# Spreading pooled k over two columns by ScalarE instead of GpSimd in a fused attention and expert kernel

## The chip, the cores and the metric

The kernel runs on one core of a Trainium2 chip. The metric is device time in microseconds (us) of one execution; runs of one kernel are told by their median. A core has five engines that work side by side, each through its own list of instructions in program order: TensorE (PE in the profile; PEld is its weight load), VectorE (DVE), ScalarE (ACT), GpSimd (POOL) and SyncE (SP), which issues the DMAs. An instruction waits on semaphores until what it needs is done, and all that stands behind it on the same engine waits too.

## The reference

Three stages stand behind each other. Attention with k and v averaged over groups of 8 positions, on 4 batches, 8 heads, 576 positions and 64 columns a head:

```python
Sp = S // pool                                   # 576 // 8 = 72 pooled positions
k_p = k.reshape(B, H, Sp, pool, D).mean(axis=3)
v_p = v.reshape(B, H, Sp, pool, D).mean(axis=3)
scores = scale * np.matmul(q, k_p.transpose(0, 1, 3, 2))
attn = softmax(scores)                           # the maximum subtracted, 1e-09 added to the sum
attn_out = np.matmul(attn, v_p)
```

Its result, as 2304 rows of 512, goes through four experts whose outputs are summed with weights: `out += p[:, e:e+1] * (np.maximum(x @ w1[e], 0) @ w2[e])`, and that through `((x @ g_w1) * (x @ g_w2)) @ g_w3 @ g_wout`. All is fp32.

## The kernel before, in words

Only the first stage and the first expert, which overlap in the first 200 us, matter here. Matrix products are done in three passes of a rounded format: a matrix is split into a high and a low half (`hi_lo`, lines 174 to 176: ScalarE copies the high half, VectorE or GpSimd subtracts it from the source for the low half), and `mm3` (lines 169 to 172) multiplies low by high, high by low and high by high.

The order of all work is written out by hand; the engines' lists follow the order in which the code records instructions. Attention is done in 18 tiles of 128 positions. A **lead** comes first: a list of pieces (lines 644 to 647) that pools k and v of batch 0, forms scores, exponents and normalised weights of tiles 0 to 2, and ends with the pooling of three chunks of k of batch 1 and with `attend(0)`, which makes the first 384 rows of x. After it the units of the first expert run: for 6 blocks of 384 rows and 8 column groups of 128, `expert_h` makes hidden values (12 matmuls, `g<-xl` and `g<-xh`; the result is copied by ScalarE, line 695, and VectorE, line 696), and two units later they are multiplied by w2 (9 matmuls, `g<-w2`). Between the units, `hooks` (lines 649 to 677) place the pieces of attention for the remaining tiles.

Pooled k of one batch is 8 heads x 72 positions = 576 rows, taken as five **chunks** (`NCH`), four of 128 rows and one of 64. `pool_k` sums a chunk's groups of eight: by one VectorE reduction (line 415), or, for chunks 0 to 2 of batch 1, by three GpSimd additions (lines 417 to 419). The sum `kp` (128x64, two buffers) is then spread to `kb` (128 x 2 x 64): each row appears in the half that belongs to its head's place in a pair of heads and is zero in the other, because the row is multiplied by the two columns of the mask `mk` (lines 349 to 356). The rows that the last chunk lacks are set to zero by GpSimd (line 413). TensorE transposes `kb` chunk by chunk (`make_kT`, line 429; in batch 0 with idle transposes between, line 432), and ScalarE copies the result from PSUM to kT (line 433). `scores` multiplies by it (line 503); VectorE takes the maximum (515) and subtracts it (520), ScalarE takes the exponent (518 in tiles 0 to 2, 521 later), VectorE sums and inverts (527 to 529), GpSimd or VectorE multiplies (532), TensorE transposes (541) and ScalarE copies (547). `attend` multiplies by pooled v (556) and splits the result into x (175, 176). After the lead all scores, transposed weights and transposes of k share two PSUM banks.

The five spreads of batch 0 stand in the lead, of batch 1 at the lead's end (chunks 0 to 2) and in hook 1 (chunks 3 and 4), of batches 2 and 3 in hooks 15 to 17 and 25 to 27, two chunks a hook.

Of the kernel before, what the change touches and what calls it, by code (L numbers as in the profile page):

```python
# [11 lines left out]
AF = mybir.ActivationFunctionType  # L12
ALU = mybir.AluOpType
# [4 lines left out]
def fused_kernel(  # L18
# [16 lines left out]
    nc = tc.nc  # L35
    PSUM = bass.MemoryType.PSUM

    B, H, S, D = q.shape
# [288 lines left out]
    with tc.manual_schedule():  # L327
# [27 lines left out]
        mk = ap.tile([P, NCH, 2], F32, tag="mk", name="mk", bufs=1)  # L355
# [37 lines left out]
        in_t, kb_t, kT_t, vp_t, qT_t, sc_t, e_t, sm_t, at_t = {}, {}, {}, {}, {}, {}, {}, {}, {}  # L393
# [13 lines left out]
        def pool_k(b, c, eng=nc.vector):  # L407
            if c == 0:
                kb_t[b] = ap.tile([P, NCH, 2, D], F32, tag="kb", name="kb", bufs=1)
            r, n = in_t.pop(("k", b, c))  # L410
            kp = ap.tile([P, D], F32, tag="kp", name="kp")
            if n < P:
                nc.gpsimd.memset(kb_t[b][n:, c], 0.0)
            if eng is nc.vector:
                eng.tensor_reduce(kp[:n], r[:n, :].rearrange("p (r d) -> p d r", d=D), axis=AX.X, op=ALU.add)  # L415
            else:
                eng.tensor_tensor(r[:n, :256], r[:n, :256], r[:n, 256:], op=ALU.add)
                eng.tensor_tensor(r[:n, :128], r[:n, :128], r[:n, 128:256], op=ALU.add)
                eng.tensor_tensor(kp[:n], r[:n, :64], r[:n, 64:128], op=ALU.add)
            nc.gpsimd.tensor_tensor(kb_t[b][:n, c], kp[:n].unsqueeze(1).broadcast_to([n, 2, D]),  # L420
                                    mk[:n, c].unsqueeze(2).broadcast_to([n, 2, D]), op=ALU.mult)

        def make_kT(b, g0, g1, warms=()):
            if g0 == 0:
# [167 lines left out]
        def do_k(b, on_pool=0):  # L592
            return [(("k", b, c), lambda c=c: pool_k(b, c, nc.gpsimd if c < on_pool else nc.vector)) for c in range(NCH)]
# [872 lines left out]
```

## Time and profile before

| | before |
|---|---|
| median of 3 runs | 1164.84 us (1162.38 to 1165.03) |
| the profiled execution | 1163.69 us |
| its span, first to last instruction | 1162.0 us |
| TensorE busy | 1152.0 us (99%) |
| VectorE busy | 795.9 us (68%) |
| GpSimd busy | 483.8 us (42%) |
| ScalarE busy | 381.4 us (33%) |

Busy time is from one execution taken by the hardware profiler. TensorE's busy time counts a matmul from its start to its end, and matmuls overlap, so a busy TensorE need not be at its peak. Idle time of an engine is put down to what released it. The shares of the whole span are means over stages that differ: the attention's pieces lie in the first 200 us.

### The profile page before, as it was taken

The page shows a single profiled execution, that of the slowest core. Times are in us where ns is not written, and L with a number is a line of the kernel's source. Part 1 is how long each engine was busy: PE and PEld are TensorE (multiplying, and loading weights), DVE is VectorE, ACT ScalarE, POOL GpSimd, SP SyncE. Part 2 cuts the span into 40 slices and gives each one's busy share as a digit, 9 for nine tenths or more (in the row PEclk, how much of TensorE's full clock was granted, in tenths as well). Part 3 has the DMA queues.
Part 4 walks back from the last instruction along what each step waited for, and adds up shares of the span by engine and source line. Part 5 has one row for each costly group of instructions (what it writes and reads, how often), then busy time and mean ns, then how long its engine had stood idle before and what let it go on. Part 6 is the DMA issues. An engine that isn't in the chain of part 4 may idle for free.

```text
span 1162.0 us, 19466 instructions
## 1 busy us (share of the span) xinstructions
PE 1152.0 (99%) x6834; PEld 1042.7 (90%) x6834; DVE 795.9 (68%) x1619; ACT 381.4 (33%) x704; POOL 483.8 (42%) x563
## 2 busy tenths in 40 slices
PE   8999999999999999999999999999999999999998
PEld 7888898999898998998989989889888999999998
DVE  6866553476586778667778577877677777775454
ACT  5543433245141234421315414124352333231110
POOL 6965222166452547634436745255001222342111
PEclk9999999999999999999999999999999999999999
DMA  8966434555877645768583488686475542945651
GB/s 212 214 151 142 143 103 143 186 194 179 284 242 219 217 135 155 225 185 253 182 251 103 154 241 246 153 269 145 138 184 210 204 165 113 329 164 187 233 190 46
DMA packets 233218, 217.54 MB, mean 187 GB/s; under 512 B 92960, under 2 KB 185376, under 8 KB 233120
## 3 DMA queue, kind: packets, MB, share of 16 engines
q1 hardware_dynamic: 233120, 216.30, 60.5%
q8 instruction: 54, 0.88, 0.3%
q14 instruction: 44, 0.36, 0.1%
HBM read 144.41 MB, written 71.83 MB: 186 GB/s over the span
## 4 chain that ended last, share of the span: by engine, by line
PE 93%; DVE 2%; DMA 2%; issue 1%; POOL 1%; ACT 1%; SPq 0%; POOLq 0%; DVEq 0%; ACTq 0%
PE g L171 17%; PE g L172 17%; PE g L170 17%; PE s L170 13%; PE s L171 13%; PE s L172 13%; PE x_ps L556 1%; PE sc L503 1%; DMA raw<-in_moe_w_dram 1%; PE at_ps L541 1%; DMA plain<-in_k_dram 0%; POOL w2l L176 0%; DVE ap L415 0%; POOL plain L841 0%; DMA stxl<-in_k_dram 0%
## 5 line engine op out<-in xcount | busy, mean ns | idle before, releaser
L176 POOL TENSOR_TENSOR round<-plain,round 128x576 fp32r<-128x576 f32 (+1 forms) x131 | 189.7, 1448 | 397.1 <-ACT round L175 269.0
L172 PE MATMUL s<-xo,wh 128*128 128x288 f32 x840 | 248.3, 296 | 0.0
L170 PE MATMUL s<-xo,wh 128*128 128x288 f32 x840 | 248.3, 296 | 0.0
L171 PE MATMUL s<-xo,wl 128*128 128x288 f32 x840 | 247.8, 295 | 0.0
L170 PE MATMUL g<-w2l,round 128*128 128x512 f32 x540 | 211.5, 392 | 0.0
L172 PE MATMUL g<-w2h,round 128*128 128x512 f32 x540 | 210.9, 391 | 0.0
L171 PE MATMUL g<-w2h,round 128*128 128x512 f32 x540 | 210.8, 390 | 0.1
L957 DVE TENSOR_TENSOR plain<-s,plain 128x288 f32<-128x288 f32 x320 | 137.9, 452 | 89.5 <-PE s L172 63.7
L170 PEld LDWEIGHTS s<-xo,wh 128*128 128x128 f32 x840 | 158.1, 188 | 0.7
L171 PEld LDWEIGHTS s<-xo,wl 128*128 128x128 f32 x840 | 157.7, 188 | 0.7
L172 PEld LDWEIGHTS s<-xo,wh 128*128 128x128 f32 x840 | 158.0, 188 | 0.0
L175 ACT ACTIVATE round<-plain 128x576 fp32r<-128x576 f32 (+1 forms) x135 | 90.9, 676 | 161.8 <-DVE plain L1315 158.7
L172 PEld LDWEIGHTS g<-w2h,round 128*128 128x128 f32 x540 | 101.3, 188 | 21.3
L170 PEld LDWEIGHTS g<-w2l,round 128*128 128x128 f32 x540 | 101.5, 188 | 20.4 <-issue 0.8
L171 PEld LDWEIGHTS g<-w2h,round 128*128 128x128 f32 x540 | 101.4, 188 | 20.1 <-DVE round L696 0.4
L959 ACT ACTIVATE plain<-s 128x288 f32<-128x288 f32 x80 | 32.2, 402 | 235.6 <-PE s L172 235.5
L1168 ACT ACTIVATE plain<-plain 128x576 f32<-128x576 f32 x96 | 65.4, 682 | 129.6 <-DVE plain L957 124.3
L288 POOL TENSOR_TENSOR x5l<-x5l 128x256 uint32<-128x256 uint32 x80 | 59.5, 744 | 101.1 <-DVE x5l L287 99.1
L957 DVE TENSOR_TENSOR plain<-s,pb 128x288 f32<-128x288 f32 x160 | 69.7, 455 | 26.0 <-PE s L172 14.5
L696 DVE SCALAR_TENSOR_TENSOR round<-g,round 128x384 fp32r<-128x384 f32 x48 | 26.6, 554 | 68.8 <-ACT round L695 68.5
L170 PE MATMUL g<-xl,round 128*128 128x384 f32 x192 | 66.6, 347 | 0.0
L172 PE MATMUL g<-xh,round 128*128 128x384 f32 x192 | 64.6, 336 | 0.0
(253 smaller groups left out, 2203.9 us busy)
## 6 DMA issues: line engine op xcount, KB each, us to landing
xo<-keptx SPq DMA_DIRECT2D x63, 576.0 KB
raw<-in_moe_w_dram SPq DMA_DIRECT2D x64, 256.0 KB
plain<-acc SPq DMA_DIRECT2D x40, 256.0 KB
keptx<-xo SPq DMA_DIRECT2D x16, 576.0 KB
x5h<-in_moe_w_dram SPq DMA_DIRECT2D x128, 64.0 KB
x5h<-in_moe_w_dram SPq DMA_DIRECT2D x32, 256.0 KB
kept<-xo SPq DMA_DIRECT2D x12, 576.0 KB
acc<-plain SPq DMA_DIRECT2D x26, 256.0 KB
```

Source lines behind the costliest of these rows:

```text
L170: nc.tensor.matmul(ps, lh, rl, start=first, stop=False)
L171: nc.tensor.matmul(ps, ll, rh, start=False, stop=False)
L172: nc.tensor.matmul(ps, lh, rh, start=False, stop=last)
L175: nc.scalar.activation(hi, src, AF.Copy)
L176: (lo_eng or nc.vector).tensor_tensor(lo, src, hi.bitcast(F32), op=ALU.subtract)
L288: nc.gpsimd.tensor_tensor(au, au, bu, op=ALU.add)
L503: nc.tensor.matmul(sc[off:off + n, (hp % 2) * W:(hp % 2 + 1) * W], qT[:, hp, off:off + n], kT_t[b][:, hp * W:(hp + 1) * W], start=True, st ...
L541: nc.tensor.transpose(pt[:NK, g * P:(g + 1) * P], e[:, half * G + g, :], ident)
L696: nc.vector.scalar_tensor_tensor(hl, ps, 0.0, hh.bitcast(F32), op0=ALU.max, op1=ALU.subtract)
L957: nc.vector.tensor_tensor(to, one, two, op=ALU.add)
L959: nc.scalar.activation(x, product(j, A11, B11), AF.Copy)
L1168: nc.scalar.activation(r, r, AF.Relu)
```

## The change

The last instruction of `pool_k`, the product of the pooled chunk with both mask columns at once on GpSimd, is replaced by two ScalarE instructions, one for each half, that copy the chunk with one mask column as a scale by row:

```diff
@@ pool_k
-            nc.gpsimd.tensor_tensor(kb_t[b][:n, c], kp[:n].unsqueeze(1).broadcast_to([n, 2, D]),
-                                    mk[:n, c].unsqueeze(2).broadcast_to([n, 2, D]), op=ALU.mult)
+            for a in range(2):
+                nc.scalar.activation(kb_t[b][:n, c, a], kp[:n], AF.Copy, scale=mk[:n, c, a:a + 1])
```

Twenty GpSimd instructions go, forty on ScalarE come. The zeroing of line 413 and the additions of lines 417 to 419 stay on GpSimd. TensorE, VectorE and SyncE keep their instructions in the same order. The number of table loads on ScalarE stays one.

On ScalarE at the start of the program, batch 0 (`pb` is the area that holds `kb`, `ap` the area of `kp` and kT), the difference, with + for what is new:

```order
 L1461 UNCONDITIONAL_BRANCH
-L433 ACT_TABLE_LOAD
+L421 ACT_TABLE_LOAD
+L421 ACTIVATE pb<-ap_70 128x64 x8
 L433 ACTIVATE ap_70<-kT_ps 128x512
+L421 ACTIVATE pb<-ap_70 64x64 x2
 L433 ACTIVATE ap_70<-kT_ps 128x128
 L487 ACTIVATE plain<-qT_ps 128x512
```

Eight copies (chunks 0 to 3) now stand ahead of the first copy of kT, and chunk 4's two stand behind it.

On ScalarE at the end of the lead and in the first units, before (`round<-raw` and `w2h<-raw` are high halves of weights, `xh<-x_ps` the high halves of the attention result, `round<-g` hidden values):

```order
L547 ACTIVATE ap_70<-at_ps 72x4x128 x5
L175 ACTIVATE round<-raw 128x512
L175 ACTIVATE xh<-x_ps 128x384 x4
L175 ACTIVATE round<-raw 128x512
L695 ACTIVATE round<-g_423 128x384
L175 ACTIVATE round<-raw 128x512
L175 ACTIVATE w2h<-raw 128x512
L521 ACTIVATE ap_70<-ap_70 128x288 x2
L695 ACTIVATE round<-g_472 128x384
```

and now, at the same place:

```order
L547 ACTIVATE ap_70<-at_ps 72x4x128 x5
L175 ACTIVATE round<-raw 128x512
L421 ACTIVATE pb<-ap_70 128x64 x6
L175 ACTIVATE xh<-x_ps 128x384 x4
L175 ACTIVATE round<-raw 128x512
L695 ACTIVATE round<-g_431 128x384
L175 ACTIVATE round<-raw 128x512
L175 ACTIVATE w2h<-raw 128x512
L521 ACTIVATE ap_70<-ap_70 128x288 x2
L421 ACTIVATE pb<-ap_70 128x64 x2
L421 ACTIVATE pb<-ap_70 64x64 x2
L695 ACTIVATE round<-g_482 128x384
```

The six copies of batch 1's chunks 0 to 2 came in between the weights and the four copies of the attention result, and the four of chunks 3 and 4 between the exponents and the second group of hidden values.

On ScalarE around batch 2, before:

```order
L175 ACTIVATE xh<-x_ps 128x384 x4
L521 ACTIVATE ap_70<-ap_70 128x288 x2
L695 ACTIVATE round<-g_903 128x384
L547 ACTIVATE ap_70<-at_ps 72x4x128 x2
L521 ACTIVATE ap_70<-ap_70 128x288 x2
L695 ACTIVATE round<-g_967 128x384
```

and now:

```order
L175 ACTIVATE xh<-x_ps 128x384 x4
L521 ACTIVATE ap_70<-ap_70 128x288 x2
L421 ACTIVATE pb<-ap_70 128x64 x4
L695 ACTIVATE round<-g_915 128x384
L547 ACTIVATE ap_70<-at_ps 72x4x128 x2
L421 ACTIVATE pb<-ap_70 128x64 x4
L521 ACTIVATE ap_70<-ap_70 128x288 x2
L421 ACTIVATE pb<-ap_70 64x64 x2
L695 ACTIVATE round<-g_982 128x384
```

The pairs of two chunks each came in ahead of the hidden values and ahead of the exponents, and chunk 4's pair ahead of the next hidden values; batch 3 has the same three places.

## Rows read from the trace of the kernel before

**Rows 1.** The page: busy us (share of the span) and instructions of each engine.

```profile
PE 1152.0 (99%) x6834; PEld 1042.7 (90%) x6834; DVE 795.9 (68%) x1619; ACT 381.4 (33%) x704; POOL 483.8 (42%) x563
```

**Rows 2.** Stretches: begin:end and length, busy us, granted clock, DMA share, GB/s.

```profile
25.90:36.00 10.10, 8.50 (x52) 7.58 (x50) 8.86 (x15) 6.36 (x13) 9.26 (x17) 1.00 0.68 178
36.00:60.00 24.00, 23.37 (x139) 20.61 (x140) 19.59 (x36) 11.66 (x24) 22.38 (x31) 1.00 0.99 222
60.00:80.00 20.00, 20.00 (x132) 17.72 (x131) 16.56 (x30) 8.84 (x19) 11.98 (x22) 1.00 0.59 124
```

**Rows 3.** Waits of TensorE: who for whom, us in total, times, longest.

```profile
PE kT_ps L429 <- POOL pb L420: 2.8, 6, 1.0
```

**Rows 4.** One line's instructions: ns least/median/most, first to last start.

```profile
L420 POOL TENSOR_TENSOR pb<-ap x20: 392/398/1422, 4.7 to 109.4; 128x128 f32<-128x128 f32 x16, 64x128 f32<-64x128 f32 x4
...
L518 ACT ACTIVATE ap<-sc,ap x24: 308/340/428, 12.1 to 18.8; 128x72 f32<-128x72 f32 x24
```

**Rows 5.** Timeline of the lead: start, us, engine, line, what [idle before <- releaser].

```profile
1.43 3.25 PE L637 MATMUL warm<-ident 128*128 128x128 f32 x14 [1.43 <-POOL ident masks.py:199]
...
9.52 0.60 ACT L433 ACTIVATE ap<-kT_ps 128x512 f32<-128x512 f32 x1 [7.42 <-PE kT_ps L429]
9.64 0.39 POOL L420 TENSOR_TENSOR pb<-ap 64x128 f32<-64x128 f32 x1 [0.28 <-DVE ap L415]
...
10.79 1.22 PE L503 MATMUL sc<-ap,plain 128*128 128x144 f32 x8
...
12.05 3.50 ACT L518 ACTIVATE ap<-sc,ap 128x72 f32<-128x72 f32 x16 [0.53 <-DVE ap L515]
...
18.70 1.47 PE L637 MATMUL warm<-ident 128*128 128x128 f32 x12
```

**Rows 6.** Timeline of the lead's end and the first expert matmuls.

```profile
22.97 0.62 ACT L175 ACTIVATE round<-raw 128x512 fp32r<-128x512 f32 x1
...
23.12 2.80 PE L556 MATMUL x_ps<-ap 72*64 72x384 f32 x16 [0.25 <-ACT ap L547]
...
24.02 1.28 POOL L176 TENSOR_TENSOR round<-raw,round 128x512 fp32r<-128x512 f32 x1
24.04 0.49 ACT L175 ACTIVATE xh<-x_ps 128x384 fp32r<-128x384 f32 x1 [0.45 <-PE x_ps L556]
...
24.56 2.49 DVE L176 TENSOR_TENSOR xl<-x_ps,xh 128x384 fp32r<-128x384 f32 x4
...
25.26 0.73 POOL L417 TENSOR_TENSOR stxh<-stxh 128x256 f32<-128x256 f32 x1
...
25.86 0.44 PE L170 MATMUL g<-xl,round 128*128 128x384 f32 x1
...
26.62 0.33 POOL L419 TENSOR_TENSOR ap<-stxh 128x64 f32<-128x64 f32 x1
...
28.04 1.14 PE L503 MATMUL sc<-ap 128*128 128x144 f32 x8
```

**Rows 7.** Timeline of the first units, with chunks 3 and 4 of batch 1.

```profile
31.77 2.03 DVE L415 TENSOR_REDUCE ap<-stxl 128x64 f32<-128x512 f32 x2
...
33.72 0.55 DVE L696 SCALAR_TENSOR_TENSOR round<-g,round 128x384 fp32r<-128x384 f32 x1
...
35.56 1.58 DVE L528 TENSOR_SCALAR ap<-ap 128x8 f32<-128x8 f32 x1
...
38.70 1.20 PE L503 MATMUL sc<-ap 128*64 128x144 f32 x16 [0.39 <-DVE ap L490]
```

**Rows 8.** Timeline of batch 2: VectorE, ScalarE and TensorE.

```profile
72.44 1.06 DVE L415 TENSOR_REDUCE ap<-stxh 128x64 f32<-128x512 f32 x1
...
72.58 1.07 ACT L547 ACTIVATE ap<-at_ps 72x512 f32<-72x512 f32 x2
...
74.87 1.14 PE L503 MATMUL sc<-ap 128*128 128x144 f32 x8
```

**Rows 9.** Stretches, as in Rows 2: the last three microseconds.

```profile
1159.00:1162.00 3.00, 0.00 (x0) 0.00 (x0) 0.23 (x1) 0.00 (x0) 0.00 (x0) 1.00 0.15 50
```

## The prediction

> **What bounds the kernel now.** I read the engine totals first, then the table of stretches, the waits of TensorE, and the timeline at the places where the changed line runs. TensorE is busy for 1152.0 us, 99% of the span [rows 1]: any time that it loses is time lost, and what another engine gains is worth only what TensorE had waited for it. The changed line runs in the first 110 us alone [rows 4]. There the stretches [rows 2] show TensorE short by 1.6 us between 25.9 and 36 us, by 0.6 us between 36 and 60, and by nothing from 60 to 80. GpSimd is the full engine of these stretches: 9.26 of 10.10 us, then 22.38 of 24.00. ScalarE has room: 6.36 and 11.66. So the change moves work from a full engine to one with room, and the waits of TensorE on that line, 2.8 us in six waits [rows 3], are the most it can give back directly.
>
> **What goes and what comes.** Twenty GpSimd products go. One takes 0.40 us by the median and 1.42 at worst [rows 4]. Forty ScalarE instructions of 128x64 (or 64x64) come, each with the mask column as a scale that is read from memory. No such row exists; the nearest is line 518, 128x72 with a bias read from memory: 0.34 us alone [rows 4], and sixteen of them in 3.50 us, so 0.22 apart [rows 5]. A pair is then 0.22 + 0.35 = 0.57 us, 0.17 more than the GpSimd product. Bounds are 0.40 (as before) and 0.68 (two without overlap); I take 0.57 because the row differs by eight columns and the source only. This matters little. What matters is the place: ScalarE works its instructions off in program order, so a pair that waits holds up all that stands behind it.
>
> **The lead, batch 0.** The pairs of chunks 0 to 3 follow VectorE's sums as the products did, each 0.17 us later. Then line 433 (the 512-column copy), which ran from 9.52 for 0.60 us, goes from 9.7 to 10.3, and the pair of chunk 4 stands behind it: it ends at 10.8, where the product ran from 9.64 to 10.03 [rows 5]. The first scores move from 10.79 to 11.55, +0.75. ScalarE carries this to line 175 (the high half of the first weights, 22.97 in [rows 6]), now about 23.7. GpSimd does not carry it: its pooling of v filled it until 24.02, so its subtraction of line 176 starts at about 24.4, +0.4.
>
> **The step that costs.** Batch 1's chunks 0 to 2 are pooled by GpSimd itself (lines 417 to 419). Their pairs now stand on ScalarE ahead of the four copies of line 175 that read the first attention result from PSUM (24.04 in [rows 6]). Before, those copies waited for nothing but TensorE. Now they wait until GpSimd has pooled three chunks. One chunk takes 1.69 us (25.26 to 26.62 + 0.33), 1.65 from start to start without the product between. With GpSimd's subtraction ending at 24.4 + 1.28 = 25.7, the third sum is ready at 25.7 + 3 x 1.65 = 30.65. The last pair adds 0.6: the first copy starts at 31.2, not at 24.04. It takes 0.49, the first low half on VectorE a quarter of 2.49, 0.62, two handovers 0.1: the first expert matmul starts at 32.45, not at 25.86, +6.6. Queued behind the waiting pairs are the copies, the high half of the second weight tile and line 695; VectorE's low halves and TensorE's whole queue wait for them. Since the low halves come 0.62 apart and TensorE takes 0.52 for each, the group ends at 34.85 at full rate, where the scores of tile 3 followed at 28.04: **+6.8**. Removing three products from GpSimd shortens this by 2 us; it is counted already.
>
> **The clock.** TensorE's last product ahead of the gap (23.12 + 2.80, moved by 0.75) ends at 26.7; it then idles for 5.8 us. At the start of the program fourteen transposes took 3.25 us, 0.23 each, and later twelve took 1.47, 0.12 each [rows 5]: after idleness the engine ran at the lower of its two levels, 1.2 GHz, though the granted-clock column prints 1.00 there too. In the last three microseconds TensorE does nothing, and the column still prints 1.00 [rows 9]. So the rows show three microseconds of idleness without a fall and a slow start after a long idleness; 5.8 us lies between. If it falls, the twelve matmuls of the first group take 0.35 each instead of 0.17: 4.16 us from 32.45, ending at 36.6, **+8.55** instead of +6.8. Bounds for this term are 0 and 3.3 us (two slow stretches like that of the start, half of each lost); I take 1.75, one stretch: 5.8 us is almost twice the idleness that did no harm, and the one start that the rows show was slow.
>
> The Trainium skill's page "TensorE: Matmul & The Clock Gate", section "Why this matters for your kernels", warns that a long idle gap between bursts of matmuls sends the array back to half rate. No row here shows a fall. By that rule the sum is the one with the fall; by [rows 9] alone it would be 1.75 us lower.
>
> **Up to the scores of tile 4.** Before, TensorE waited here for chunks 2, 3 and 4: 1.6 us. Chunks 0 to 2 are now ready before TensorE comes to them. Chunks 3 and 4 are summed by VectorE (31.77 for 2.03 us [rows 7], now about 40.2 to 42.2), and their pairs stand on ScalarE ahead of line 695 of the second group: 42.2 + 0.6 = 42.8, then 0.49, so VectorE's line 696, which stood at 33.72, comes at 43.25, +9.5. From there to the scores of tile 4 were 4.98 us (33.72 to 38.70), of which over 1.0 was in one tiny VectorE instruction, line 528, that lasted 1.58 us [rows 7] beside a busy GpSimd. With GpSimd freer I give 1.0 back: 47.2, **+8.5**; if not, 48.2, +9.5. So the 1.6 us that TensorE gains is given back to a new wait on the scores.
>
> **Batches 2 and 3.** VectorE sums all five chunks. The pairs of chunks 0 and 1 now stand ahead of line 695, and so of line 547, which empties two PSUM banks (72.58, 1.07 us [rows 8]). The second sum ends at 73.50; pair 0.6, line 695 0.4: line 547 runs from 74.5 to 75.6. The next scores need these banks at 74.87 and, for the second half, at 75.3: 0.25 to 0.3 us of wait. In batch 2 the same happens once more ahead of the transposes of k, because three large copies stand behind chunk 4's pair: 0.3. Together **+0.8**; bounds 0 (the slack of two units holds) and 2. The 0.6 us that TensorE missed between 36 and 60 may come back in part: -0.3.
>
> **The sum.** 8.5 + 0.8 - 0.3 = +9.0 on the profiled execution's 1163.69 us (span 1162.0 and 1.7 around it), 1172.7. That execution lies 1.15 below the median of the runs shown, 1164.84, and inside their spread, so I leave it so.
>
> **Rivals.** *The clock holds*: all as above without 1.75 us: +7.25, 1170.9. For it: three idle microseconds at full clock in [rows 9]; against it: the gap is twice as long.
>
> *The gap is made up*: the head start of the weight loads during the gap and a GpSimd with 8 us less work (20 x 0.40) would let later stages catch up. TensorE's misses after 25.9 are 1.6 + 0.6 us before 60 and none up to 80, so at most 2.2 of the gap come back, if the clock holds and the new waits all vanish: 6.6 - 2.2 = +4.4, 1168.1. Against it: TensorE has no idleness to give.
>
> *The wait spreads*: each pair waits for VectorE, VectorE waits for line 695 behind it, and a loop of waits costs every unit of batches 1 to 3 a microsecond: some 6 more, +15, 1178. Against it: [rows 2] leave ScalarE half its time from 36 to 60, and two groups of matmuls lie between a result and its use.
>
> *Faster*: GpSimd's load is what decides, and the copies of the attention result do not wait. This decides if the third pooled chunk is ready when ScalarE comes to the copies, at 24.04; then TensorE's 2.8 us [rows 3] go and the pairs cost 0.75 in the lead: -2, 1161.7. GpSimd only begins the first chunk at 25.26 and needs 5 us for three, so this is out by 6.6 us.
>
> **How the numbers follow.** The forecast 0.60; the clock holds 0.20; made up 0.10; spreads 0.07; faster 0.03. The range is 1168 to 1177: at the lower end the clock holds, batches 2 and 3 cost nothing, and 2 us more come back, which takes in half of the made-up case; at the upper end 1.0 (line 528), 1.2 (batches) and 1.5 (a second slow stretch) come on top of the forecast, with 0.6 more in the lead (pairs without overlap). That leaves out less than 0.2: the other half, the spreading waits and the faster case. A measurement of this kernel tells about 0.3% (3.5 us) from no change. Faster by more than that 0.02, within it 0.07 (the rest of the faster case and half of made up), slower 0.91.
>
> **What would show it.** In the profile after: ScalarE idle from about 24.4 to 30.6, released by GpSimd's line 419 in three steps; the copies of line 175 at 31; TensorE idle for almost 6 us just before its first expert matmul, at 32 to 33; those first matmuls 0.35 apart (clock fell) or 0.17 (held); no wait of TensorE on the transposes of batch 1; a wait of 1 to 3 us on the scores of tile 4; GpSimd busy 8 us less or more. I am wrong if the copies start before 28, or if TensorE's busy time plus its gaps does not grow by about the gap.

## The result

The changed kernel took **1172.23 us** (median of 4 runs, 1171.37 to 1174.04); the kernel before took 1164.01 beside it on the same chip (4 runs, 1162.38 to 1165.03). The ratio is 1.0074, 95% interval 1.0062 to 1.0087: slower, by 8.2 us. The forecast was 1172.7, and slower by more than 0.3% with a chance of 0.91. The profiled execution took 1172.54 us, its span is 1170.5.

The page of the changed kernel, engine totals, against [rows 1]: GpSimd has 9.3 us less to do, ScalarE 9.2 more, and TensorE is as full as before.

```profile
PE 1153.6 (99%) x6834; PEld 1044.8 (89%) x6834; DVE 794.5 (68%) x1619; ACT 390.6 (33%) x744; POOL 474.5 (41%) x543
```

The new line as a group of instructions (ns least/median/most, first to last start), against [rows 4]. The price of one is 0.336 us, and nearly constant; the GpSimd product's went up to 1.42.

```profile
L421 ACT ACTIVATE pb<-ap x40: 332/336/352, 4.5 to 118.2; 128x64 f32<-128x64 f32 x32, 64x64 f32<-64x64 f32 x8
```

Waits of TensorE, then of ScalarE, in the first 125 us of the changed kernel (who for whom: us in total, times, longest), against [rows 3]:

```profile
PE g L170 <- DVE xl L176: 6.1, 1, 6.1
PE kT_ps L429 <- ACT pb L421: 2.5, 5, 0.8
PE sc L503 <- DVE ap L490: 1.9, 1, 1.9
```

```profile
ACT pb L421 <- DVE ap L415: 14.5, 16, 2.5
ACT pb L421 <- POOL ap L419: 5.7, 3, 3.4
```

TensorE's wait for the spread, which the change could have taken away, is still there (2.5 us after 2.8): of it 1.9 us lie in batch 0 and 0.6 at the last chunk of batch 1, where 1.2 and 1.6 lay before. A new wait of 6.1 us stands ahead of the first expert matmul, and ScalarE waits 5.7 us in three steps for GpSimd's last additions. The timeline of the lead's end shows how the two are one thing (start, us, engine, line, what, [idle before <- releaser]), against [rows 6]:

```profile
23.45 0.62 ACT L175 ACTIVATE round<-raw 128x512 fp32r<-128x512 f32 x1
...
23.61 2.80 PE L556 MATMUL x_ps<-ap 72*64 72x384 f32 x16 [0.24 <-ACT ap L547]
...
24.52 1.27 POOL L176 TENSOR_TENSOR round<-raw,round 128x512 fp32r<-128x512 f32 x1
...
27.44 0.59 ACT L421 ACTIVATE pb<-ap 128x64 f32<-128x64 f32 x2 [3.37 <-POOL ap L419]
27.64 0.72 POOL L417 TENSOR_TENSOR stxh<-stxh 128x256 f32<-128x256 f32 x1 [0.24 <-DMA stxh<-in_k_dram]
...
29.32 0.59 ACT L421 ACTIVATE pb<-ap 128x64 f32<-128x64 f32 x2 [1.30 <-POOL ap L419]
...
30.57 0.32 POOL L419 TENSOR_TENSOR ap<-stxh 128x64 f32<-128x64 f32 x1
30.93 0.59 ACT L421 ACTIVATE pb<-ap 128x64 f32<-128x64 f32 x2 [1.02 <-POOL ap L419]
31.42 1.61 ACT L175 ACTIVATE xh<-x_ps 128x384 fp32r<-128x384 f32 x4
31.92 1.95 DVE L176 TENSOR_TENSOR xl<-x_ps,xh 128x384 fp32r<-128x384 f32 x4 [6.79 <-ACT xh L175]
...
32.53 0.69 PE L170 MATMUL g<-xl,round 128*128 128x384 f32 x1 [6.13 <-DVE xl L176]
...
36.54 0.85 PE L503 MATMUL sc<-ap 128*128 128x144 f32 x5
```

TensorE's attention result lies ready from 26.4 us. ScalarE has nothing to do but the three pairs, and these wait for GpSimd until 30.9; the copies of the result stand behind them. TensorE does nothing from 26.4 to 32.5.

The stretches of the changed kernel (begin:end and length, busy us of PE, PEld, DVE, ACT, POOL, granted clock, DMA share, GB/s), against [rows 2]:

```profile
29.00:30.00 1.00, 0.00 (x0) 0.00 (x0) 0.00 (x0) 0.59 (x2) 0.97 (x2) 0.93 0.27 78
30.00:31.00 1.00, 0.00 (x0) 0.00 (x0) 0.00 (x0) 0.07 (x1) 0.77 (x2) 0.50 0.39 90
32.50:36.00 3.50, 3.47 (x11) 3.47 (x12) 1.97 (x4) 1.04 (x3) 0.00 (x0) 0.50 0.15 21
36.00:44.50 8.50, 7.94 (x47) 7.38 (x46) 6.11 (x11) 5.29 (x13) 1.63 (x3) 0.96 0.58 151
44.50:60.00 15.50, 13.60 (x86) 12.12 (x85) 13.88 (x26) 7.25 (x16) 14.31 (x20) 1.00 0.84 207
60.00:80.00 20.00, 20.00 (x134) 17.85 (x133) 14.79 (x30) 9.67 (x20) 14.07 (x20) 1.00 0.80 182
```

The granted clock is 1.00 up to a little before 30 us and 0.50 from there (1.2 GHz, the lower level), still in the gap; the first eleven matmuls run at 0.50, and 36.0 to 44.5 has 0.96. The Trainium skill's page "TensorE: Matmul & The Clock Gate", section "Why this matters for your kernels", warns that a long idle gap between bursts sends the array back to half rate; this trace agrees, with 6.1 idle us and a fall in them. The runs below show that the length of the gap alone does not tell it.

The timeline of the first units, against [rows 7]:

```profile
42.22 0.59 ACT L421 ACTIVATE pb<-ap 64x64 f32<-64x64 f32 x2 [0.38 <-DVE ap L415]
...
43.21 0.56 DVE L696 SCALAR_TENSOR_TENSOR round<-g,round 128x384 fp32r<-128x384 f32 x1 [1.03 <-ACT round L695]
...
44.36 1.29 POOL L176 TENSOR_TENSOR w2l<-raw,w2h 128x512 fp32r<-128x512 f32 x1 [4.42 <-issue]
...
45.12 0.55 DVE L528 TENSOR_SCALAR ap<-ap 128x8 f32<-128x8 f32 x1
...
47.23 1.04 PE L503 MATMUL sc<-ap 128*64 128x144 f32 x13 [1.90 <-DVE ap L490]
```

To see where the time comes from, take the same matmul of TensorE in both traces and subtract the starts; the difference is the shift. The scores of tile 3 come 8.5 us later (28.04 and 36.54), those of tile 4 also 8.5 (38.70 and 47.23), the scores that stood at 55.60 come 8.1 later, those at 104.79 8.4 later, and the last matmul 8.6. Between, it falls to 7.3 (32.64 and 39.93), where TensorE no longer waits for the transposes, and the wait on the scores of tile 4 puts it back. So the whole loss is made by 37 us, and little comes or goes after 48 in these two executions.

### The profile page after: what moved, and what is told of

Same layout as the page of the kernel before. It is cut to its first block, busy times and chain, and to the rows that moved or that the text cites. A ratio compares the mean times of both kernels' runs of the same rounds, so it can differ in the third digit from the quotient of the medians.

```text
span 1170.5 us, 19486 instructions
## 1 busy us (share of the span) xinstructions
PE 1153.6 (99%) x6834; PEld 1044.8 (89%) x6834; DVE 794.5 (68%) x1619; ACT 390.6 (33%) x744; POOL 474.5 (41%) x543
## 4 chain that ended last, share of the span: by engine, by line
PE 93%; DMA 2%; DVE 2%; SPq 1%; issue 1%; POOL 1%; ACT 1%; ACTq 0%; POOLq 0%; DVEq 0%
PE g L171 17%; PE g L172 17%; PE g L170 17%; PE s L170 13%; PE s L171 13%; PE s L172 13%; PE sc L503 1%; PE x_ps L556 1%; PE at_ps L541 1%; DMA stxl<-in_v_dram 0%; SPq L472 0%; DMA stxh<-in_k_dram 0%; DMA stxh<-in_v_dram 0%; SPq L460 0%; SPq L404 0%
```

## The experiments

Theory: the three pairs of batch 1 stand on ScalarE ahead of copies that have nothing to do with them, wait there for GpSimd's pooling, and that one wait, with the clock that falls in it, is the loss. Rival: the spread costs more on ScalarE wherever it stands. A further rival for the size: the gap is all, and the clock costs nothing. Each edit is shown against the changed kernel (but for the kernel with the pairs in hook 0, which starts from the kernel before); `...` stands for lines or arguments left out. Where a condition chooses which chunks ScalarE spreads, the others are spread by GpSimd's product as before. The edits move line numbers: lines 490, 503, 520 and 528 of the kernel before are 494, 507, 524 and 532 in the kernels with such a condition. "Later" is always the start of the same TensorE matmul less that in the kernel before.

### Three pairs alone

ScalarE spreads chunks 0 to 2 of batch 1; the other seventeen spreads are GpSimd's again.

```diff
+            if b == 1 and c < 3:
+                for a in range(2):
+                    nc.scalar.activation(kb_t[b][:n, c, a], ...)
+            else:
+                nc.gpsimd.tensor_tensor(kb_t[b][:n, c], ...)
```

> Only the three chunks of batch 1 that GpSimd pools itself are spread by ScalarE; the other seventeen stay on GpSimd. Theory (wait): the loss is one wait, that of the attention result's copies behind these three pairs, so nearly all of it is here: first expert matmul at about 32.0 us, low clock behind it, 1171 to 1172 us. Rival (price): each pair is dearer than the product and pays its share of 8.2 us, 0.41 a pair: three pairs, +1.2, 1165.2.

Measured 1170.79 us (the kernel before beside it: 1164.33), ratio 1.0053 [1.0038, 1.0068]: 6.5 us of the 8.2 come with three of the twenty pairs, a little less than the 1171 to 1172 expected and far above the rival's 1165.2. The wait of the changed kernel is there, and the granted clock stands at 0.50 behind it, from 32 to 36 us (waits of TensorE in this kernel, first 125 us):

```profile
PE g L170 <- DVE xl L176: 5.8, 1, 5.8
```

### All but these three

```diff
+            if not (b == 1 and c < 3):
...
```

> The opposite: seventeen chunks on ScalarE, the three of batch 1 that GpSimd pools on GpSimd. Wait theory: the lead is 0.5 us later, chunks 3 and 4 of batch 1 hold up the second hidden group, batches 2 and 3 cost 0.2 to 0.8: 1165 to 1166.3, first expert matmul at 26.4 us. Price rival: seventeen pairs at 0.41, +7, 1171.

Measured 1165.92 us, ratio 1.0013 [1.0003, 1.0022]: 1.6 us for seventeen pairs. The rival of the price (1171) falls here too. The two parts add up to 8.1 us, the whole change to 8.2.

This kernel has no gap ahead of the first expert matmul, and yet its trace shows the low clock once. The waits of TensorE, then stretches:

```profile
PE sc L507 <- DVE ap L494: 1.9, 1, 1.9
```

```profile
39.00:40.00 1.00, 0.00 (x0) 0.00 (x0) 1.00 (x2) 0.28 (x2) 0.94 (x1) 1.00 1.07 203
40.00:41.00 1.00, 0.77 (x8) 0.80 (x10) 1.00 (x3) 0.00 (x0) 0.92 (x3) 0.66 1.12 221
41.00:43.50 2.50, 2.50 (x16) 2.12 (x13) 2.27 (x5) 0.49 (x2) 2.42 (x4) 0.50 1.06 216
```

A wait of 1.9 us on the scores of tile 4 was followed by the lower level, though TensorE had already gone on. In that execution the scores of tile 4 were 1.5 us later and the next scores 3.1. It took 1167.23 us, more than the median. The record has ten executions of this kernel with their mean granted clock: the five at 1.000 took 1164.76 to 1165.93 us (median 1165.51), the five at 0.998 or 0.999 1165.92 to 1167.48 (median 1167.04). So here a lower mean clock goes with some 1.5 us to the end of the program; it is a difference between executions, not an experiment.

### Batch 0 alone, and batches 2 and 3 alone

```diff
+            if b == 0:
...
```

> ScalarE spreads the five chunks of batch 0 alone; all others on GpSimd as before. By the prediction's terms: the first scores 0.7 later, the second weight's subtraction on GpSimd 0.4 later, the three pooled chunks of batch 1 and the wait for them 0.4 later, so +0.5 on the kernel before, not to be told from no change. Rival, that the cost lies evenly over the pairs (8.2 us by 5 of 20): +2.1.

Measured 1165.38 us (12 runs; before 1164.02), ratio 1.0013 [1.0005, 1.0022]: +1.4 us. The interval, 0.6 to 2.6 us, just leaves out the theory's +0.5 and holds the rival's +2.1, so the expectation missed: a cost of batch 0 is clear of noise. That the cost lies evenly over all pairs is out by the other runs; for these five it isn't. In the profiled execution TensorE waited less for the spread and more behind it (waits of TensorE, first 125 us):

```profile
PE sc L507 <- DVE ap L494: 1.7, 1, 1.7
PE kT_ps L433 <- ACT pb L422: 1.4, 2, 0.8
...
PE kT_ps L433 <- POOL pb L424: 0.6, 1, 0.6
```

```diff
+            if b >= 2:
...
```

> Only batches 2 and 3 (ten chunks) are spread by ScalarE; batches 0 and 1 by GpSimd as before. The forecast gave these +0.8; the changed kernel's trace, read from the scores of tile 6 to those of batch 3, gives +0.3: 1164.3 + 0.3 = 1164.6. Price rival, 0.41 a pair: 1168.4.

Measured 1165.62 us (10 runs; before 1164.22), ratio 1.0008 [0.9999, 1.0018]. By the medians that is +1.4 us, by the interval -0.1 to +2.1. The trace, of an execution that took 1163.97 us, 1.7 less than the median, shows the shift of TensorE grow from 0.2 to 0.7 us over batches 2 and 3 and fall to 0.3 at the end, with two waits on line 524 (line 520 of the kernel before), 0.6 us together. Whether the time is 0.3, 0.8 or 1.4 longer, the runs don't tell; the rival's 4.1 is out.

### The pairs behind the copies, and one pair ahead of them

If the place is what costs, moving the three pooled chunks behind `attend(0)` in the lead takes the wait away while ScalarE does the same work.

```diff
-                + weight(GP) + do_qT(3) + k1[:3] + do_attend(0) + weight(VE))
+                + weight(GP) + do_qT(3) + do_attend(0) + k1[:3] + weight(VE))
```

> As the changed kernel, but the three chunks of batch 1 are recorded behind attend(0): the copies of the attention result stand ahead of the pairs again. Wait theory: the gap ahead of the first expert matmul goes (26.4 us), but the same wait now holds the second weight tile and the first hidden group's copy until about 32.0 to 32.5, and from there VectorE's chain to the scores of tile 4 is as long as in the changed kernel (9.9 us): scores at 42.7 instead of 47.2, +4.0, 1168. Rival (the gap is all): the time falls back to 1164.5.

Measured 1167.75 us, ratio 1.0029 [1.0019, 1.0039]: 4.5 us less than the changed kernel and 3.4 more than the kernel before, near the 1168 of the theory; the rival's 1164.5 is out. The first expert matmul isn't held up any more (26.82 us), but the second weight tile now stands behind the pairs, and the scores of tile 4 come at 42.39 (42.7 expected). Waits of TensorE, then two stretches:

```profile
PE g L170 <- ACT round L175: 1.8, 1, 1.8
...
PE sc L503 <- DVE ap L490: 1.2, 1, 1.2
```

```profile
33.00:34.00 1.00, 1.00 (x6) 1.00 (x5) 1.00 (x3) 0.34 (x1) 0.59 (x1) 0.67 0.86 239
34.00:36.00 2.00, 2.00 (x8) 1.91 (x7) 1.93 (x5) 0.89 (x2) 1.04 (x2) 0.50 0.65 189
```

With one pair left ahead of the copies and two behind:

```diff
+                + weight(GP) + do_qT(3) + k1[:1] + do_attend(0) + k1[1:3] + weight(VE))
```

> As the changed kernel, but only chunk 0 of batch 1 is recorded ahead of attend(0), chunks 1 and 2 behind it. Theory (what counts is when the third pair lets line 695 of the first hidden group go, not the length of the gap): the first expert matmul starts at about 29.1 us, between 26.8 (all three behind) and 32.5 (all three ahead), but line 696 of the first group is as late as with all three behind, so the time is that of that run, 1167.8, +3.4. Rival (the gap itself is the loss): a gap of 2.5 us more than with all three behind, 1170.

Measured 1168.11 us, ratio 1.0039 [1.0025, 1.0052]. Waits of TensorE, and the two stretches behind the gap:

```profile
PE g L170 <- DVE xl L176: 2.3, 1, 2.3
PE sc L503 <- DVE ap L490: 1.9, 1, 1.9
```

```profile
26.00:29.00 3.00, 0.73 (x5) 0.47 (x4) 1.08 (x3) 2.07 (x7) 2.72 (x6) 1.00 0.71 149
29.00:40.00 11.00, 10.17 (x57) 8.83 (x56) 8.43 (x15) 7.73 (x22) 3.71 (x6) 1.00 0.68 169
```

One pair costs a gap of 2.3 us where three cost 6.1, and the time is that of the kernel with all three behind the copies, as the theory has it; the rival's 1170 lies just below the interval's upper end (1170.3), so the time alone doesn't rule it out, but the last matmul comes 3.8 us late in both. The clock holds here through the gap of 2.3 us and through the wait of 1.9, while waits of 1.8 (pairs behind the copies) and 1.9 (all but three) were followed by a fall.

### Idle transposes in the gap

To keep the clock up and leave the wait as it is, 44 idle transposes (`warm`) stand behind `attend(0)`, and in a second kernel 16 more ahead of the scores of tile 4.

```diff
+                + weight(GP) + do_qT(3) + k1[:3] + do_attend(0) + warm(44) + weight(VE))
```

> The changed kernel with 44 idle transposes (4.8 us at 0.109) on TensorE in the gap ahead of the first expert matmul. Theory (the clock adds 1.75 us to the wait): granted clock 1.00 throughout, the first group's matmuls 0.17 apart, scores of tile 3 at 34.8 instead of 36.5, scores of tile 4 at 45.5 instead of 47.2, time 1170.4. Rival (VectorE and ScalarE set the pace there, the clock costs nothing): scores of tile 4 stay at 47.2, 1172.2.

Measured 1173.64 us (1171.91 to 1173.87; the profiled execution is the fastest), ratio 1.0075 [1.006, 1.009]: no gain. In the profiled execution the clock held through the gap and fell at the next wait, behind the scores of tile 4. Why the other three took 1.7 to 2.0 us longer than it, the trace can't show.

```profile
26.00:44.00 18.00, 15.54 (x104) 14.13 (x102) 10.64 (x19) 10.87 (x28) 7.04 (x12) 1.00 0.64 149
44.00:46.00 2.00, 1.39 (x14) 1.42 (x16) 2.00 (x4) 0.00 (x0) 1.92 (x3) 0.71 1.02 238
46.00:48.00 2.00, 2.00 (x10) 1.62 (x7) 1.55 (x4) 0.73 (x2) 1.92 (x4) 0.50 0.74 206
```

Then both gaps:

```diff
+        hooks[at[TPB + 1]][:0] = warm(16)
```

> The changed kernel with idle transposes on TensorE in both of its waits: 44 ahead of the first expert matmul and 16 (1.75 us) ahead of the scores of tile 4. In the run with the first 44 alone the low level only moved: it stood 3.4 us behind the scores of tile 4 instead of 4.2 us of work behind the gap. Theory (the low level is what costs): no low stretch from 20 to 60 us, scores of tile 4 at 44.6 and full rate behind them, 1170.0 to 1170.5. Rival (the time is set by VectorE's chain, the low level is only seen beside it): 1172 to 1173.6, as with the first 44.

Measured 1171.56 us, ratio 1.0063 [1.005, 1.0077], an interval that overlaps the changed kernel's. It reaches from 1170.0 to 1173.2 us, which holds both the theory's time and the lower part of the rival's, so this run decides nothing; all four of its times, 1171.09 to 1171.75, lie between the two. The same kernel and the changed one were then run side by side, five times each:

> The changed kernel once more, beside the next one on the same chip. Every theory: 1171.4 to 1174, as when it was timed first; scores of tile 4 near 47.2 us, a low level of the clock behind 29.9 us.

> The kernel with idle transposes in both gaps once more, beside the changed kernel. Theory that the low level of the clock is paid once and kept to the end: 1.8 us less than the changed kernel in the same call, both in the median and in the shift of TensorE's last matmuls. Rival, that a later wait takes it back (as the 1.2 us near 322 us did in the first execution): medians less than 1 us apart, though the shift up to 105 us is 1.8 us or more smaller. If the interval of the two overlaps and the late wait is absent, neither is shown.

Changed kernel 1171.69 us, ratio 1.0071 [1.0059, 1.0083]; both gaps warm 1171.83 us, 1.0068 [1.0056, 1.008]. Stretches of the changed kernel in this execution:

```profile
27.00:36.00 9.00, 5.03 (x18) 5.04 (x19) 2.82 (x6) 4.00 (x11) 2.09 (x5) 0.62 0.37 94
36.00:45.50 9.50, 7.54 (x43) 6.50 (x41) 8.26 (x15) 6.28 (x16) 3.81 (x4) 1.00 0.73 162
45.50:49.50 4.00, 3.84 (x22) 3.49 (x23) 3.02 (x7) 0.89 (x2) 3.84 (x6) 0.57 0.87 212
```

and of the kernel with both gaps warm:

```profile
27.00:36.00 9.00, 7.35 (x57) 7.12 (x55) 3.48 (x7) 5.25 (x14) 3.20 (x7) 1.00 0.53 135
36.00:45.50 9.50, 8.68 (x60) 7.74 (x60) 8.26 (x15) 5.61 (x15) 4.45 (x5) 1.00 0.83 187
45.50:49.50 4.00, 4.00 (x30) 3.62 (x26) 2.72 (x6) 1.76 (x4) 3.71 (x6) 1.00 0.59 179
```

From the first expert matmul to the scores of tile 4 the changed kernel takes 14.70 us in its first execution and 14.69 in its second; with the gap warm it takes 12.88, and with both 12.92 and 12.91. So the lower level costs 1.8 us there: the two executions with the fall and the three without it differ by that. It is complete at the scores of tile 3 (4.01 and 4.00 us with the fall, 2.22, 2.22 and 2.20 without). In these two runs the scores that stood at 104.79 come 8.4 us late in the changed kernel and 6.3 with both gaps warm. But then the saving shrinks: the kernel with both gaps warm, in both of its executions, meets one more wait near 329 us (waits of TensorE, 300 to 340 us):

```profile
PE s L170 <- DVE plain L1240: 0.6, 1, 0.6
```

There VectorE's chain of another stage, which works on tiles that arrive by DMA, comes last. The end is 7.7 us late against 8.6. The medians lie 0.14 us apart, as the rival has it, and the late wait is there, of 0.6 or 0.9 us; that it alone takes the saving back isn't shown, for it is smaller than 1.8. Why VectorE is late there only in this kernel, and where the rest goes between the profiled executions and the medians, stays open.

### The pairs in the first hook

This starts from the kernel before: only the three pooled chunks are spread by ScalarE, in hook 0, behind the copies and behind the second weight tile; the sums get a third buffer.

```diff
+            if b == 1 and c < 3:
+                kp_t[c] = kp
+                return
...
+        def spread_k(c):
+            for a in range(2):
+                nc.scalar.activation(kb_t[1][:, c, a], kp_t[c], AF.Copy, scale=mk[:, c, a:a + 1])
...
+        hooks[0] = [(None, lambda c=c: spread_k(c)) for c in range(3)]
```

> The kernel before, with one edit: chunks 0 to 2 of batch 1 are pooled by GpSimd in the lead, but spread by ScalarE only in hook 0, behind the first hidden group's copy and the first w2 weights, with a third buffer for the sums. No copy waits for GpSimd, and GpSimd has three products less ahead of chunks 3 and 4. Theory: TensorE's wait for chunk 2 shrinks from 1.0 to 0.1 to 0.4, those for chunks 3 and 4 (0.6) go, the scores of tile 4 come about 1 us earlier: 1163.0 to 1163.5, 0.9987 to 0.9993. Rival (VectorE's chain sets the scores of tile 4 whatever GpSimd does): no change, 1164.3.

Measured 1164.47 us (11 runs; before 1164.22), ratio 1.0007 [0.9998, 1.0016]. The theory's gain isn't there, and the rival is right in the number. The scores of tile 4 come 0.6 us earlier than before, but the same scores come 0.7 earlier (37.98) in the kernel with batches 2 and 3 alone, which up to there is the kernel before; so the 0.6 can't be put down to the edit. In that kernel's trace VectorE's line 528 (532 there), 1.58 us long in [rows 7], took about half:

```profile
35.58 0.84 DVE L532 TENSOR_SCALAR ap<-ap 128x8 f32<-128x8 f32 x1
```

The scores at 55.60 come 0.7 later with the pairs in hook 0. The timeline of ScalarE shows a wait for a weight tile there, where the kernel before copied the same tile at 47.99 us right behind its other work. Why the tile came later, and whether this is the whole of the 0.7 us, isn't shown:

```profile
49.59 0.63 ACT L175 ACTIVATE round<-raw 128x512 fp32r<-128x512 f32 x1 [2.17 <-DMA raw<-in_moe_w_dram]
```

So in a place where they wait for nothing the three pairs cost nothing that the runs can tell (0.3 us), against 6.5 us in the changed place; no gain shows either. No version here beats the kernel before.

## Why the prediction was right

**The lead.** First scores +0.67 us for +0.75; GpSimd's subtraction of line 176 at 24.52 for 24.4. A pair took 0.59 for 0.57 (a single one 0.336). But that the first scores met the term so closely is chance: in the second execution of the changed kernel they came 0.4 us earlier than before. Over the nine traces in which ScalarE spreads batch 0 they came at 10.36 to 12.47 us, 11.38 in the mean; over the four in which GpSimd does, at 10.47 to 11.00, 10.80 in the mean. That is +0.6 for +0.75, right in the mean; single executions differ by more.

**The step that costs.** Third sum at 30.89 (30.57 + 0.32) for 30.65, the first copy at 31.42 for 31.2, the first expert matmul at 32.53 for 32.45. The number is better than its terms. The second chunk waited 0.24 us for its DMA, which the forecast had not, and the other two took 1.61 and 1.60 for 1.65. From the first copy to the first expert matmul it took 1.11 us, not 1.25, since the first low half took 0.49 and not 0.62. These offset each other in part. Three pairs alone give 6.5 of the 8.2 us, and the same pairs in hook 0 give 0.3 that can't be told from nothing: that their place is what costs is shown, not only argued. The *faster* rival fell as it was said to: the third pooled chunk was 6.8 us late for 24.04.

**The clock.** Forecast +1.75, measured 1.8 in the stretch, and the fall lies inside the gap, so *the clock holds* fell; in all three executions with a gap of over 5 us (6.1, 5.8 and 5.5) the clock fell in it. What the forecast set against it, three idle microseconds at 1.00 in [rows 9], carries little: by the prediction's own reading the column prints 1.00 at the start of the program too, where the engine ran slow. The scores of tile 3 came at 36.54 for 36.6. But the step is shown for this stretch alone: for the end of the program the runs with idle transposes don't show that it costs anything that isn't taken back later, while the ten executions of the kernel with all but three pairs speak for a cost that stays. This is open. Nor does a gap alone decide it: the second execution of the changed kernel started 1.6 us better (first expert matmul at 30.97), fell once more at 45.5 to 49.5, and ended 8.6 us late like the first. The bound of 1.5 us for a second slow stretch, meant for the upper end of the range, was met there.

**Up to the scores of tile 4.** 43.21 for 43.25 on line 696, 47.23 for 47.2 on the scores. The 1.6 us that TensorE had to gain became the 1.9 us wait on line 490, VectorE's, as written, but for one sign that failed: a wait of TensorE on the transposes of batch 1 stayed, 0.56 us for chunk 4. The 1.0 us that was given back came too, line 528 taking 0.55 instead of 1.58, but not for the reason given, that GpSimd was freer. It was idle for 4.4 us ahead, yet beside line 528 it ran the same subtraction in both kernels (timeline of GpSimd, before):

```profile
35.82 1.29 POOL L176 TENSOR_TENSOR w2l<-raw,w2h 128x512 fp32r<-128x512 f32 x1
```

Before, line 528 ended at 37.14 and this subtraction at 37.11; in the changed kernel they ended at 45.67 and 45.65. Line 528 ended with it each time, and only began closer to its end. The number was right by where the two happened to meet. The 1.58 itself is of one execution: with batches 2 and 3 alone, the same code up to there took 0.84.

**Batches 2 and 3.** By the traces this term was mis-sized: +0.8 was put, and the shift grew from 8.1 to 8.4, +0.3, and no wait of TensorE shows from 60 to 135 us where waits of about 0.3 were forecast. With batches 2 and 3 alone the shift at the end is 0.3 too. Both lie between the bounds of this term, near the lower one. By the medians of that kernel it is +1.4 with an interval that holds all of 0, 0.3 and 0.8, so its size stays open. The -0.3 for the 0.6 us that TensorE missed between 36 and 60 came as -0.4.

**The sum.** +9.0 was put on the profiled execution, +8.9 was measured between the two (+8.6 at the last matmul); between the medians it is +8.2. *Made up* (+4.4) and *the wait spreads* (+15) fell: from the scores of tile 4 on, the shift stayed between 8.1 and 8.6. One part did not behave alone as its term said: batch 0 alone cost 1.4 us by the medians. Its profiled execution had the first scores 1.7 us late, against +0.7 and -0.4 in the two of the changed kernel, so the start of the program differs between executions of one kernel by more than this term; in the changed kernel's time it can't be seen. So that the sum came within 0.5 us of the measured median is luck in part: the mechanism and its main term are right, but smaller terms were off both ways, and the second execution reached the same 8.6 us with another lead and a second slow stretch.

## What to carry to other kernels

Before work is moved to an engine with room, read what stands behind its new place on that engine and when its inputs are ready: an instruction that waits costs the whole queue behind it, and busy shares do not show this. Three of twenty pairs made four fifths of the loss, by one wait of 6 us. Moved only behind the copies, they still held up the weights behind them (with the other seventeen pairs in it, 3.4 us were left of the 8.2); behind those too, they cost nothing that could be told. A wait removed at one place (1.0 of 1.6 us here) is only worth what the next wait leaves of it, so follow the same matmul through both traces to the end of the stage.

## What the runs showed of the hardware

- The granted clock fell in gaps of 6.1, 5.8 and 5.5 us, held in one of 2.3, and fell behind waits of 1.8 and 1.9 us in other kernels. The changed kernel shows both at the same place: behind its wait of 1.9 us on the scores of tile 4 the clock was 1.00 in the first execution and fell in the second (0.57 from 45.5 to 49.5 us). The idle time just ahead does not tell it.
- A fall in the gap itself costs nothing there; it is paid when TensorE goes on. Eleven matmuls of 128x384 started 0.32 us apart at 0.50 (33.02 to 36.22 us in the changed kernel), where starts lie 0.17 to 0.18 apart at 1.00.
- The tiny VectorE instruction of line 528 (128x8) takes 0.17 us in most tiles, but 1.58 before and 0.55 in the changed kernel in the tile told of above; both times it ended 0.02 to 0.03 us after a GpSimd subtraction of 128x512 that ran beside it. Batch 0 alone shows a third: 37.39 to 38.14, the subtraction ending at 38.11. It is the same in all thirteen traces (the line is 532 or 537 where an edit moved it): of its 234 runs 160 took 0.17 to 0.18 us, and each of the 74 others, 0.20 to 1.58 us long, began beside a running GpSimd instruction and ended 0.03 us after one. The reciprocal behind it, line 529, of the same shape, took 0.20 to 0.21 us each time, 38 times of 234 beside a GpSimd instruction that ran all through it. The Trainium skill's page "SBUF — State Buffer", section "Who interferes with whom", has a rule that would give it: VectorE and GpSimd share one pair of ports, whoever has it keeps it for a whole instruction, and `tensor_scalar`, the operation of line 528, can be among those that want it. The 74 endings agree with that; no run here tested it.
